# Sparse attention with a gated feed-forward on one core: first gate weights in one transfer, and the head of the written-out order rewritten

## The chip, the cores and the metric

The kernel runs on one core of a Trainium2 chip. A core has a matrix engine (TensorE, PE in the profile, with its weight loads shown apart as PEld), three engines for elementwise work (VectorE or DVE, ScalarE or ACT, GpSimd or POOL), and SyncE (SP), which here only issues transfers. Each engine has a queue of its own and runs it in order; engines wait for each other by semaphores. Sixteen DMA engines move data between the chip's memory and the core. They serve several queues; in the profile, q1 holds the transfers that SP issues and q0 those that POOL issues.

The metric is the device time of one execution in microseconds. Lower is better.

## The reference

Causal attention in which each query attends only to the six chunks of 32 keys whose scores have the highest upper bound, and then a gated feed-forward over all tokens:

```python
k_min = np.min(k_chunks, axis=3)
k_max = np.max(k_chunks, axis=3)
ub = np.sum(np.maximum(q[:, :, :, None, :] * k_min[:, :, None, :, :],
                       q[:, :, :, None, :] * k_max[:, :, None, :, :]), axis=-1)
ub = np.where(causal, ub, -1000000000.0)
top_chunks = np.argsort(ub, axis=-1)[..., -6:]
...
scores = np.where(sel & (pos[:, None] >= pos[None, :]), scale * q @ k.T, -1000000000.0)
attn = softmax(scores)
x = (attn @ v) as [3072 tokens, 512]
gate = 1 / (1 + exp(-(x @ w_gate)))
out = ((gate * (x @ w_val)) @ w_out)
```

There are 4 batches, 8 heads, 768 positions and a head dimension of 64, so x has 3072 rows of 512. The feed-forward has 1536 columns. Inputs and output are fp32; the kernel computes in fp16 with fp32 sums.

## The kernel before

The work is cut into eight units, u0 to u7, of 384 tokens each. Unit u0 takes the first 128 queries of batches 0, 1 and 2. These lie in the first four chunks, so all of their allowed chunks are selected and no choice is needed. The function `first` does them, one batch at a time, under names that end in the batch: `kf0_0`, `kf1_0` (loads of even and odd heads' keys), `qf0_0`, `qf1_0`, `vf_0`; `kfT_0`, `qfT_0` (transposes on TensorE, L709), `kf16_0`, `qf16_0` (casts), `scf_0` (scores, L746), `expf` (ACT, L751), `cmf` (causal mask on POOL, L753), `vc_1`, `vc_2` (values cast to fp16 as `vh`), `pvf` (weights times values, L760), `rzf` and `xf` (division by the sum, DVE, L766 and L768), `xpsf` (turned back, L775) and `xTf` (copied to the feed-forward's input). Unit u1 is the other half of the start, queries 128 to 511 of batch 0. Its loads (`k0_u1` to `k3_u1`, `q0_u1` to `q3_u1`, L647, one for each pair of heads) are copied (`kn`, `qn`), turned (`kT`, `qT`, L795), cast (`kt`, `qf`) and spread into per-head tiles (`hk0`, `hk1`, `hq0`, `hq1`). `kx0` and `kx1` (L681) are the minimum and maximum over each chunk, `kcr` the range between them, `qm` the positive part of the queries, `ub` the upper bounds on TensorE (L896); from them a choice is made on DVE, and then scores, exponentials and values follow as in u0. Raw values for u1 come by `v_0_1` to `v_0_3` (L667), cast on POOL by `v16`.

The tiles of keys and queries have rows of a fixed pattern that is copied into them once from `epat` (`hkp` copies, eight of them).

The feed-forward of a unit (`ffn`, L1239 to L1319) has 12 column blocks: four matmuls for the gate `g` (128x384 each, L1259), tanh on ACT, four matmuls for the value `v`, one product on DVE (`hg`, L1280), and in the end matmuls with `w_out` (`o`, L1308). u0's block starts as soon as u0's attention is done, and u1's attention is woven into it. All weights are loaded in that time, cast to fp16 by the transfer, by POOL's queue: gate, value and output weights each in three groups of four blocks (`wg0` to `wg2`, L612; `wv0` to `wv2`, L613; `wo0` to `wo2`). Only the first gate group is split: `wgp` (L610) brings the first 128 rows of its 512, and `wg0` the other 384.

At the very start and between the early steps stand 30 matmuls on a tile of ones (`fl_0` to `fl_29`, L591), whose result nobody reads; they keep TensorE occupied. Before the change, nine of them run first and the others stand between transposes up to the start of the feed-forward.

The order of all work is written out. `ORDER` is one list of about 2010 operations; each entry names an operation and its engine (`P` TensorE, `A` ACT, `V` DVE, `G` POOL, `S` SP), and each engine's queue holds its entries in the order of that list. `SLOTS` gives each buffer the place that it takes in its pool. `TIES` holds extra waits: `a<b` makes `a` wait for `b` although no data passes between them. The loop at the end of the kernel emits the operations:

```python
    for op in plan.order():
        n = len(traced)
        op.emit(op.engine)
        for b in ties.get(op.name, ()):
            tc.add_manual_dep(traced[n], ends[b], ...)
```

Loads come in the order of SP's entries. Before, they are: `k2_u1 qf1_0 kf1_0 kf0_0 kf1_2 kf0_1 qf0_0 qf1_1 kf1_1 qf0_1 vf_0 qf0_2 qf1_2 kf0_2 vf_1 k0_u1 q3_u1 q2_u1 vf_2 q1_u1 k3_u1 q0_u1 k1_u1 v_0_3 v_0_2 v_0_1 qf1_3 k0_u2 q2_u2 k1_u2`, and then the rest of u2's and batch 3's first block.

Of the kernel before, what the change touches and what calls it, by code (L numbers as in the profile page):

```python
# [401 lines left out]
def kernel(  # L402
# [201 lines left out]

    def weights(i, prio, after):
        lo, hi = 512 * i, 512 * i + 512
        c0 = 0
        if i == 0:
            c0 = 1
            plan.add("wgp", {POOL: (760, 760)}, lambda e: nc.gpsimd.dma_start(wg16[:, 0:1, lo:hi], wgs[:, 0:1, lo:hi]),  # L610
# [846 lines left out]
```

## Time and profile before

| | |
|---|---|
| median of 3 runs | 280.38 us (279.79 to 280.73) |
| the profiled execution's own time | 279.88 us |
| its span in the profile | 278.2 us |
| granted TensorE clock, mean | 1.000 of full |
| TensorE busy | 269.2 us, 97% |
| DVE, ACT, POOL busy | 231.2, 180.4, 163.1 us |
| moved by DMA | 34.70 MB, mean 125 GB/s |

The span runs from the first to the last instruction that the profile shows; the execution's time has 1.7 us more around it. "Busy" is the time in which an engine has an instruction in work, so a busy TensorE isn't one at its peak rate. A row of the groups, such as `L1259 PE MATMUL g_u<-xT_u,wg 128*128 128x384 f16 x288 | 56.0, 326 | ...`, gives line, engine, operation, output and inputs, the shape and count, total busy us, mean ns of one, and the idle time just ahead of them with what ended it. A row of the timeline gives start, length (both us), engine, line and operation, and how many of them follow each other; in brackets stands how long the engine had been idle and what released it. In the answers on waits the three numbers are the total, the times and the longest. In the chain that ended last, a row is a start, a length, and what the time was spent on. A row on transfers gives the queue, the count of issues, the size of one, and the median time from the start of its issue to its landing.

### The profile page before, as it was taken

The numbers are of one execution on the slowest core, as the hardware profiler recorded it, in microseconds if no ns is written. First come the engines' busy times: TensorE is split into PE (matmuls) and PEld (weight loads), VectorE is DVE, ScalarE is ACT, GpSimd is POOL, SyncE is SP. The second block draws the span as 40 slices with busy tenths as digits, with TensorE's granted clock in tenths as the row PEclk, the third lists the DMA queues.
The fourth block names the chain that finished last, engine by engine and source line by source line (L and its number), as shares of the span: only waits on it lengthen the run. The fifth ranks groups of instructions, "written<-read, shape, count | busy, mean of one in ns | idle before, by whom it ended". The sixth has DMA issues, their size and how long they took to land.

```text
span 278.2 us, 7566 instructions
## 1 busy us (share of the span) xinstructions
PE 269.2 (97%) x2806; PEld 189.3 (68%) x2806; DVE 231.2 (83%) x686; ACT 180.4 (65%) x386; POOL 163.1 (59%) x262
## 2 busy tenths in 40 slices
PE   5979999999999999999999999999999999999995
PEld 3755658667755666557687657776888688778684
DVE  4799747687999998796999987978889998888985
ACT  6388969569858944468689979988983422341430
POOL 5797744639372873534669966724766467163440
PEclk9999999999999999999999999999999999999999
DMA  6999999999999598696896230100320033000304
GB/s 157 258 281 204 207 217 208 220 179 202 187 217 189 142 183 188 145 161 125 164 157 114 68 85 17 40 0 3 73 77 2 1 83 127 2 1 2 151 2 152
DMA packets 131717, 34.70 MB, mean 125 GB/s; under 512 B 119776, under 2 KB 128736, under 8 KB 131680
## 3 DMA queue, kind: packets, MB, share of 16 engines
q1 hardware_dynamic: 126912, 29.50, 50.6%
q0 software_dynamic: 4768, 4.72, 10.1%
q8 instruction: 22, 0.36, 0.5%
q14 instruction: 15, 0.12, 0.1%
HBM read 30.67 MB, written 6.29 MB: 133 GB/s over the span
## 4 chain that ended last, share of the span: by engine, by line
PE 87%; DMA 6%; DVE 5%; SPq 1%; issue 0%; POOL 0%; DVEq 0%
PE v_u L1259 20%; PE g_u L1259 15%; PE sc_u L957 12%; PE o_u L1308 11%; PE p_u L1082 10%; PE pv_u L990 7%; DMA wg<-in_moe_w_gate_dram 5%; PE p_g_u L1191 5%; PE ube_u L896 3%; DMA kf<-in_k_dram 1%; DVE xf L768 1%; PE kfT L709 1%; PE qfT L709 1%; PE fl L591 1%; DVE kx_u L681 1%; DVE kcr L681 1%
## 5 line engine op out<-in xcount | busy, mean ns | idle before, releaser
L968 ACT ACTIVATE att_u<-sc_u 128x512 f16<-128x512 f32 (+3 forms) x184 | 86.9, 573 | 8.6 <-PE sc_u L957 7.3
L1259 PE MATMUL v_u<-xT_u,wv 128*128 128x384 f16 x384 | 72.4, 326 | 0.0
L1280 DVE SCALAR_TENSOR_TENSOR hg_u<-gate_u,v_u 128x384 f16<-128x384 f16 x96 | 51.2, 545 | 19.3 <-ACT gate_u L1271 9.7
L1271 ACT ACTIVATE gate_u<-g_u 128x384 f16<-128x384 f32 x72 | 35.1, 499 | 40.3 <-PE g_u L1259 35.1
L1259 PE MATMUL g_u<-xT_u,wg 128*128 128x384 f16 x288 | 56.0, 326 | 0.9 <-ACT xT_u L452 0.5
L1259 PEld LDWEIGHTS <-wv 128*128 128x128 f16 x384 | 36.2, 98 | 20.3 <-issue 0.2
L974 POOL TENSOR_SCALAR_AFFINE_SELECT att_u<-att_u 128x384 f16<-128x384 f16 (+1 forms) x56 | 28.0, 509 | 37.4 <-ACT att_u L968 16.4
L1259 PEld LDWEIGHTS <-wg 128*128 128x128 f16 x288 | 26.7, 98 | 18.3 <-DMA wg<-in_moe_w_gate_dram 1.8
L1308 PE MATMUL o_u<-wo,hg_u 128*128 128x512 f16 x144 | 34.3, 379 | 0.0
L990 PE MATMUL pv_u<-v,att_u 128*128 128x65 f16 x640 | 26.3, 193 | 0.0
L990 PEld LDWEIGHTS <-att_u 128*128 128x128 f16 x640 | 24.2, 98 | 2.9 <-issue 0.6
L1228 DVE TENSOR_TENSOR f_g_u<-p_g_u,f_g_u 128x192 f32<-128x192 f32 (+1 forms) x72 | 24.9, 383 | 1.0 <-PE p_g_u L1191 0.4
L957 PE MATMUL sc_u<-hqe,hke 128*128 128x128 f16 (+2 forms) x220 | 25.1, 243 | 0.0
L957 PE MATMUL sc_u<-hqo,hko 128*128 128x128 f16 (+2 forms) x220 | 24.1, 243 | 0.0
L1308 PEld LDWEIGHTS <-hg_u 128*128 128x128 f16 x144 | 13.7, 98 | 13.4
L957 PEld LDWEIGHTS <-hke 128*128 128x128 f16 x220 | 16.5, 98 | 4.9 <-issue 0.6
L957 PEld LDWEIGHTS <-hko 128*128 128x128 f16 x220 | 16.4, 98 | 4.4
L673 POOL CAST v<-v 128x512 f16<-128x512 f32 x23 | 14.4, 627 | 5.8 <-DVE qf_u L863 1.8
L1271 ACT ACTIVATE gate_u<-f_g_u 128x384 f16<-128x384 f32 x24 | 11.9, 519 | 5.6 <-DVE hg_u L1280 2.9
L1011 DVE TENSOR_TENSOR x_u<-pv_u,rz_u 128x384 f16<-128x384 f32 (+1 forms) x28 | 14.6, 524 | 0.9 <-DMA xT_u<-x_u 0.6
L919 DVE MAX8 mx_u<-ubn_u 128x8 f32<-128x8 f32 (+16 forms) x152 | 12.7, 158 | 0.3
L1099 DVE SCALAR_TENSOR_TENSOR sw<-p_u,sw 128x256 f32<-128x256 f32 (+1 forms) x20 | 10.6, 528 | 2.4 <-PE p_u L1082 2.0
(187 smaller groups left out, 504.9 us busy)
## 6 DMA issues: line engine op xcount, KB each, us to landing
v<-in_v_dram SPq DMA_DIRECT2D x23, 256.0 KB, 4.7
k<-in_k_dram SPq DMA_DIRECT2D x12, 384.0 KB, 5.4
q<-in_q_dram SPq DMA_DIRECT2D x12, 384.0 KB, 5.9
out_dram<-osb_u SPq DMA_DIRECT2D x12, 256.0 KB, 3.3
out_dram<-sw SPq DMA_DIRECT2D x8, 256.0 KB, 2.1
wv<-in_moe_w_val_dram POOLq DMA_DIRECT2D x3, 512.0 KB, 9.8
wo<-in_moe_w_out_dram POOLq DMA_DIRECT2D x3, 512.0 KB, 17.6
qf<-in_q_dram SPq DMA_DIRECT2D x8, 128.0 KB, 3.3
```

What stands on the lines that cost most here:

```text
L673: plan.add(f"v16_{b}_{ib}", {POOL: pool(H * D)}, lambda e: nc.gpsimd.tensor_copy(v16[b % 2][:, ib, :, 0:D], at(t)), reads=[t], writes=[("v ...
L957: nc.tensor.matmul(at(t)[:, o:o + 128 * m], hk[b % 2][e_][:, p, 128 * jb:128 * jb + 128], hq[u.side][e_][:, p, 128 * x:128 * (x + m)], sta ...
L968: plan.add(f"exp_{u.name}_{h}_{y}", {ACT: act(n)}, lambda e, t=t, att=att, b0=b0, n=n: nc.scalar.activation(at(att)[:, b0:b0 + n], at(t), ...
L974: nc.gpsimd.affine_select(out=dv, in_=dv, compare_op=ALU.is_ge, fill=0.0, base=0, pattern=[[0, u.m], [1, 128]], channel_multiplier=-1)
L990: nc.tensor.matmul(at(pv)[:, last, x, :], at(att)[:, c:c + 128], v16[b % 2][:, jb, h, :], start=(jb == 0), stop=(jb == ib))
L1011: plan.add(f"x_{u.name}_{p}", {DVE: dve(u.t)}, lambda e: nc.vector.tensor_tensor(at(x_).rearrange("p a (e d) -> p e a d", e=2), at(pv)[:, ...
L1082: nc.tensor.matmul(at(to)[:, side], a(j)[:, i], b(j)[:, i], start=j == i == 0, stop=j == 2 and i == 1)
L1228: plan.add(f"{p}_{name}", {POOL: pool2(192 * n), DVE: dve(192 * n)} if slow else {DVE: dve(192 * n)}, lambda e: both(e).tensor_tensor(dst( ...
L1259: nc.tensor.matmul(at(t), w16[:, c, 128 * fb:128 * fb + 128], at(u.xt)[:, c, :], start=(c == 0), stop=(c == 3))
L1271: plan.add(f"tanh_{u.name}_{fb}", {ACT: act(T, not seven[0])}, lambda e, gv=gv, gate=gate: nc.scalar.activation(at(gate), gv(), AF.Tanh, s ...
L1280: plan.add(f"hg_{u.name}_{fb}", {DVE: dve(T)}, lambda e, vv=vv, gate=gate, hg=hg, fb=fb: nc.vector.scalar_tensor_tensor(at(hg)[:, fb % 2], ...
L1308: nc.tensor.matmul(at(o), at(hgs[fc // 2])[:, fc % 2, 128 * tb:128 * tb + 128], wo16[:, fc, lo:hi], start=(fc == 0), stop=(fc == NFB - 1))
```

## The change

The change rewrites the first 290 or so entries of `ORDER` (the rest, 1717 entries, stays the same), renumbers `SLOTS`, adds six `TIES` and loads the first gate group in one transfer. In parts:

- **Gate weights.** `wgp` is gone; `wg0` brings all 512 rows (512 KB in fp16). The gate matmuls of the first four blocks no longer read the separate part. On POOL, `wg0` and `wv0` now stand ahead of the key copy `hkf0` and behind `cmf_1_1`, as the list shows.
- **Loads.** SP's order is now `k2_u1 kf1_2 kf0_0 kf1_0 qf1_0 qf0_1 qf0_0 qf1_1 qf1_2 qf0_2 kf0_2 kf0_1 kf1_1 vf_0 vf_1 k0_u1 q3_u1 k3_u1 v_0_2 vf_2 q2_u1 q1_u1 k1_u1 q0_u1 v_0_3 v_0_1 qf1_3 k0_u2 k1_u2 q2_u2`, and the rest as before.
- **Fillers.** 28 of the 30 matmuls on ones stand at the start of TensorE's queue, ahead of the first transpose; one follows the first key transpose and one stands ahead of `scf_1`. None is left behind that.
- **Order on TensorE.** Batch 2's first block is turned ahead of batch 1's; the feed-forward begins with `g_u0_2 g_u0_0`, then `ub_u1`, `g_u0_1 g_u0_3` and the value blocks 1, 3, 2, 0 (before: `g_u0_0 g_u0_2`, `ub_u1`, `g_u0_3 g_u0_1`, and the value blocks 1, 0, 2, 3).
- **Engines.** 28 copies and casts run elsewhere. DVE to ACT: `kt_u1_2 kf16_0 kf16_1 kn_u1_0 xTf_1_1 qf_u1_1 qf_u1_2 hkp001 hkp101 hq1_u1_0 hkf1`. DVE to POOL: `kcr_f`. ACT to DVE: `kn_u1_2 hkp110 hkp000 hk1_u1_2 hkp111 qn_u1_0 kt_u1_3 hq0_u1_2`. ACT to POOL: `qm_u1_3 qm_u1_2 hq1_u1_1`. POOL to ACT: `hk0_u1_2 hkp100 vc_2 hk0_u1_3 hq1_u1_3`.
- **Ties.** `kcr_f<rzf_2_1 hkf0<rzf_2_0 kn_u1_1<xf_2_0 qm_u1_3<kx0_u1_3 hq0_u1_3<qn_u1_0 hq1_u1_1<hq0_u1_2`, all on POOL, waiting for DVE. No old tie is gone.

The diff, without the renumbered slots and the rewrapped lists:

```diff
@@ ORDER @@
-ident=G ones16=V fl_4=P fl_2=P fl_8=P fl_3=P fl_1=P fl_0=P fl_29=P k2_u1=S kn_u1_2=A qf1_0=S kf1_0=S kf0_0=S fl_6=P fl_5=P epat0=V
-ident16=V ap0=V epat=G hkp110=A hkp000=A hkp001=V kT_u1_2=P kcr0=V kt_u1_2=V hk0_u1_2=G vf1_1=G hkp011=V hkp010=G vf1_2=G hkp100=G
-kf1_2=S kf0_1=S kfT_0=P kxf1=V fl_17=P fl_10=P fl_7=P kx0_u1_2=V kf16_0=V qf0_0=S qfT_0=P qf16_0=V qf1_1=S kf1_1=S kfT_1=P
-kf16_1=V fl_15=P fl_16=P scf_0=P expf_0_1=A fl_19=P qf0_1=S qfT_1=P hq0=V ap1=V fl_14=P fl_9=P fl_13=P fl_11=P fl_18=P fl_12=P
-qf16_1=V scf_1=P v10=G vf_0=S v16_0_0=G qf0_2=S qf1_2=S kf0_2=S expf_0_0=A cmf_0_0=G pvf_0_0=P rzf_0_0=V xf_0_0=V kx1_u1_2=V
-cmf_0_1=G wgp=G kfT_2=P pvf_0_1=P qfT_2=P qf16_2=V rzf_0_1=V xf_0_1=V kxf0=V expf_1_0=A cmf_1_0=G vf_1=S vc_1=G pvf_1_0=P
-rzf_1_0=V xpsf_0_0=P expf_1_1=A cmf_1_1=G pvf_1_1=P hkf0=G hk1_u1_2=A kf16_2=A scf_2=P expf_2_1=A expf_2_0=A k0_u1=S kn_u1_0=V
-kT_u1_0=P xf_1_0=V fl_20=P fl_21=P wg0=G q3_u1=S qn_u1_3=A q2_u1=S rzf_1_1=V xf_1_1=V xpsf_1_1=P hq1=V xTf_1_1=V kx0_u1_0=V
-kx1_u1_0=V vf_2=S wv0=G cmf_2_0=G fl_23=P xpsf_0_1=P fl_24=P fl_22=P fl_27=P xpsf_1_0=P vc_2=G xTf_1_0=V pvf_2_0=P rzf_2_0=V
-xf_2_0=V q1_u1=S k3_u1=S kn_u1_3=G kT_u1_3=P hkp111=A q0_u1=S fl_28=P kx1_u1_3=V cmf_2_1=G pvf_2_1=P xpsf_2_0=P rzf_2_1=V xf_2_1=V
-qT_u1_3=P qf_u1_3=V k1_u1=S qn_u1_1=A qT_u1_1=P xTf_0_0=A xTf_0_1=A qn_u1_2=A qn_u1_0=A kn_u1_1=G kT_u1_1=P kx1_u1_1=V kx0_u1_1=V
-kt_u1_0=A qm_u1_3=A fl_25=P xpsf_2_1=P fl_26=P qT_u1_2=P v_0_3=S v_0_2=S v_0_1=S qf1_3=S k0_u2=S q2_u2=S k1_u2=S qf_u1_1=V
-qf_u1_2=V v11=G wv1=G wg1=G hq0_u1_3=G qT_u1_0=P kt_u1_3=A hk0_u1_3=G hq1_u1_3=G wv2=G xTf_2_1=A xTf_2_0=A qf_u1_0=A qm_u1_0=A
-g_u0_0=P g_u0_2=P kx0_u1_3=V kcr_f=V kcr_u1=V hkp101=V hq1_u1_0=V hkf1=V kt_u1_1=V hk0_u1_1=G wg2=G qm_u1_2=A qm_u1_1=A ub_u1=P
-ubn0_u1=V ubm0_u1=V hq0_u1_1=A hq0_u1_2=A g_u0_3=P g_u0_1=P mx0_u1=V ap0_u1=V apt0_u1=V hqm0_u1_0=V v_u0_1=P v_u0_0=P v_u0_2=P
-hq0_u1_0=A tanh_u0_2=A tanh_u0_1=A hg_u0_1=V ubn1_u1=V v_u0_3=P tanh_u0_3=A hg_u0_3=V ubm1_u1=V hg_u0_2=V tanh_u0_0=A hg_u0_0=V
-hk0_u1_0=A hq1_u1_1=A sc_u1_0_2=P exp_u1_0_2=A sc_u1_1_2=P sc_u1_0_1=P sc_u1_0_0=P exp_u1_1_2=A sc_u1_1_0=P sc_u1_1_1=P
-exp_u1_0_0=A exp_u1_0_1=A v_u0_7=P wo0=G hqm0_u1_2=G sc_u1_2_2=P exp_u1_2_2=A sc_u1_2_0=P exp_u1_2_0=A sc_u1_3_0=P sc_u1_3_2=P
...
+ones16=V fl_23=P k2_u1=S kf1_2=S fl_4=P fl_12=P fl_10=P ident=G epat0=V epat=G hkp000=V hkp100=A hkp001=A ap0=V kn_u1_2=V v11=G
+hkp010=G kf0_0=S kf1_0=S qf1_0=S qf0_1=S fl_15=P fl_24=P fl_28=P fl_19=P fl_2=P fl_17=P fl_9=P fl_0=P fl_20=P fl_26=P fl_27=P
+fl_6=P fl_18=P fl_1=P fl_22=P fl_5=P fl_25=P fl_8=P fl_29=P fl_11=P fl_14=P fl_7=P fl_13=P fl_3=P kT_u1_2=P kt_u1_2=A hk0_u1_2=A
+fl_16=P hkp110=V hkp111=V kfT_0=P qf0_0=S qfT_0=P ident16=V qf16_0=V hkp011=V kf16_0=A scf_0=P expf_0_1=A kcr0=V hk1_u1_2=V
+kx1_u1_2=V qf1_1=S qfT_1=P cmf_0_1=G expf_0_0=A cmf_0_0=G qf1_2=S qf0_2=S qfT_2=P kf0_2=S kfT_2=P kf16_2=A kf0_1=S kf1_1=S kfT_1=P
+kf16_1=A qf16_1=V qf16_2=V fl_21=P scf_1=P expf_1_0=A vf_0=S v10=G v16_0_0=G pvf_0_0=P rzf_0_0=V pvf_0_1=P rzf_0_1=V xf_0_0=V
+xpsf_0_0=P xf_0_1=V xpsf_0_1=P vf1_1=G vf_1=S vc_1=G cmf_1_0=G pvf_1_0=P expf_1_1=A cmf_1_1=G vf1_2=G wg0=G k0_u1=S q3_u1=S
+k3_u1=S xTf_0_0=A qn_u1_3=A wv0=G scf_2=P expf_2_1=A expf_2_0=A kxf1=V kxf0=V kx0_u1_2=V rzf_1_0=V pvf_1_1=P rzf_1_1=V xf_1_1=V
+v_0_2=S vf_2=S q2_u1=S xpsf_1_1=P ap1=V xf_1_0=V xpsf_1_0=P qT_u1_3=P qf_u1_3=V hkf1=A xTf_0_1=A xTf_1_1=A cmf_2_0=G cmf_2_1=G
+vc_2=A pvf_2_1=P rzf_2_1=V pvf_2_0=P rzf_2_0=V xf_2_1=V xf_2_0=V xTf_1_0=V kn_u1_0=A kT_u1_0=P kx1_u1_0=V wv1=G kn_u1_3=G
+kT_u1_3=P kx0_u1_3=V kx1_u1_3=V kx0_u1_0=V kt_u1_3=V xpsf_2_1=P xpsf_2_0=P q1_u1=S qn_u1_1=A qT_u1_1=P hq1_u1_3=A qn_u1_2=A
+hkp101=A xTf_2_0=A qf_u1_1=A qT_u1_2=P qf_u1_2=A kt_u1_0=A xTf_2_1=A qm_u1_1=A kcr_f=G k1_u1=S hkf0=G kn_u1_1=G kT_u1_1=P wg1=G
+qm_u1_3=G q0_u1=S qn_u1_0=V qT_u1_0=P qf_u1_0=A qm_u1_0=A g_u0_2=P g_u0_0=P wv2=G hq0_u1_3=G qm_u1_2=G kx1_u1_1=V hq0=V kx0_u1_1=V
+kcr_u1=V ub_u1=P kt_u1_1=V hq0_u1_2=V ubn0_u1=V ubm0_u1=V hq0_u1_0=A wg2=G hq1_u1_1=G mx0_u1=V ap0_u1=V apt0_u1=V hqm0_u1_0=V
+hk0_u1_0=A g_u0_1=P g_u0_3=P hq1_u1_0=A v_u0_1=P tanh_u0_1=A hg_u0_1=V ubn1_u1=V hq0_u1_1=A tanh_u0_3=A v_u0_3=P hg_u0_3=V
+ubm1_u1=V v_u0_2=P tanh_u0_2=A hg_u0_2=V hq1=V v_u0_0=P tanh_u0_0=A hg_u0_0=V hk0_u1_3=A sc_u1_0_2=P exp_u1_0_2=A hk0_u1_1=G
+sc_u1_1_2=P sc_u1_0_1=P sc_u1_0_0=P exp_u1_1_2=A sc_u1_1_0=P sc_u1_1_1=P exp_u1_0_0=A exp_u1_0_1=A v_u0_7=P wo0=G hqm0_u1_2=G
...
@@ TIES, first line of the new list @@
+kcr_f<rzf_2_1 hkf0<rzf_2_0 kn_u1_1<xf_2_0 qm_u1_3<kx0_u1_3 hq0_u1_3<qn_u1_0 hq1_u1_1<hq0_u1_2 hqm0_u1_2<hqm0_u1_0 v16_0_3<hg_u0_1
...
@@ -604,13 +604,8 @@
 
     def weights(i, prio, after):
         lo, hi = 512 * i, 512 * i + 512
-        c0 = 0
-        if i == 0:
-            c0 = 1
-            plan.add("wgp", {POOL: (760, 760)}, lambda e: nc.gpsimd.dma_start(wg16[:, 0:1, lo:hi], wgs[:, 0:1, lo:hi]),
-                     writes=[("wg", 0, "first")], prio=prio, dma=(750, 2048))
-        return plan.add(f"wg{i}", {POOL: (760, 760)}, lambda e: nc.gpsimd.dma_start(wg16[:, c0:, lo:hi], wgs[:, c0:, lo:hi]),
-                 reads=after, writes=[("wg", i)], prio=prio, dma=(750 * (4 - c0), 2048)), plan.add(f"wv{i}", {POOL: (760, 760)}, lambda e: nc.gpsimd.dma_start(wv16[:, :, lo:hi], wvs[:, :, lo:hi]),
+        return plan.add(f"wg{i}", {POOL: (760, 760)}, lambda e: nc.gpsimd.dma_start(wg16[:, :, lo:hi], wgs[:, :, lo:hi]),
+                 reads=after, writes=[("wg", i)], prio=prio, dma=(3000, 2048)), plan.add(f"wv{i}", {POOL: (760, 760)}, lambda e: nc.gpsimd.dma_start(wv16[:, :, lo:hi], wvs[:, :, lo:hi]),
                  reads=after, writes=[("wv", i)], prio=prio, dma=(3000, 2048))
 
@@ -1265,7 +1260,7 @@
             else:
                 g = ps(f"g_{u.name}_{fb}", "ff", [128, T])
                 gv, gk = lambda g=g: at(g), [g]
-                op = plan.add(f"g_{u.name}_{fb}", pe(650), product(g, wg16), reads=xt + [("wg", fb // 4)] + [("wg", 0, "first")] * (fb < 4), writes=[g],
+                op = plan.add(f"g_{u.name}_{fb}", pe(650), product(g, wg16), reads=xt + [("wg", fb // 4)], writes=[g],
                               prio=next_())
                 plan.hold(op, gate)
             plan.add(f"tanh_{u.name}_{fb}", {ACT: act(T, not seven[0])}, lambda e, gv=gv, gate=gate: nc.scalar.activation(

```

220 lines of the change are left out of this document (110 added, 110 removed).

## The prediction

> **What bounds the kernel now.** I read the page's shares first, then busy time by stretch, then what TensorE waits for in the first 50 us, and then the early rows one by one.
>
> ```profile
> span 278.2 us, 7566 instructions
> PE 269.2 (97%) x2806; PEld 189.3 (68%) x2806; DVE 231.2 (83%) x686; ACT 180.4 (65%) x386; POOL 163.1 (59%) x262
> ```
> ```profile
> 14.00:18.00 4.00, 2.39 (x32) 1.65 (x31) 3.65 (x12) 2.83 (x6) 4.00 (x7) 1.00 1.14 298
> 18.00:23.00 5.00, 4.05 (x40) 3.10 (x37) 4.93 (x14) 4.95 (x12) 4.79 (x11) 1.00 1.25 233
> 23.00:40.00 17.00, 16.88 (x156) 10.25 (x155) 12.06 (x49) 13.20 (x33) 9.60 (x17) 1.00 1.21 209
> 40.00:60.00 20.00, 19.75 (x216) 13.05 (x215) 14.47 (x54) 13.87 (x36) 10.32 (x21) 1.00 1.12 206
> ```
> ```profile
> PE g_u L1259 <- ACT xT_u L452: 0.5, 1, 0.5
> PE g_u L1259 <- DMA wg<-in_moe_w_gate_dram: 0.2, 1, 0.2
> ```
>
> The first line of the page's shares is busy time. In the rows by stretch, columns after the stretch and its length are busy us of PE, weight load, DVE, ACT and POOL, then clock, DMA share, GB/s. TensorE is busy 97% of the span and has almost no hole after 23 us, so what the change can move is when the first feed-forward block (unit u0) begins on it, and any hole that it opens or shuts later. The order of the work after the first 290 operations is the same in both kernels. Only three things of the new head reach past 23 us: the start of that block, the landings of the weights, and the landings of the loads queued behind them. The one wait still shown there, 0.2 us, is for the last gate weights. Between 14 and 23 us four engines are all nearly full, POOL 4.00 of 4.00, DVE 4.93 of 5.00: whatever is put there displaces something.
>
> **The change, part by part.**
>
> *Gate weights in one transfer.* POOL issues them:
>
> ```profile
> 12.82 0.79 POOL L610 DMA_DIRECT2D wg<-in_moe_w_gate_dram  x1
> 13.63 0.66 POOL L753 TENSOR_SCALAR_AFFINE_SELECT attf<-attf 128x512 f16<-128x512 f16 x1
> 14.21 0.63 POOL L456 CAST vh<-vf 128x512 f16<-128x512 f32 x1
> 14.77 0.64 POOL L753 TENSOR_SCALAR_AFFINE_SELECT attf<-attf 128x512 f16<-128x512 f16 x1
> 15.35 0.61 POOL L456 COPY hke<-kf 64x512 f16<-64x512 f16 x1
> 15.91 0.80 POOL L612 DMA_DIRECT2D wg<-in_moe_w_gate_dram  x1
> ```
> ```profile
> wg<-in_moe_w_gate_dram POOLq DMA_DIRECT2D x1, 128.0 KB, 5.5
> ```
> ```profile
> wg<-in_moe_w_gate_dram POOLq DMA_DIRECT2D x1, 384.0 KB, 7.3
> ```
>
> The small issue (0.79 us of POOL) goes, and the key copy `hkf0` (0.61) moves behind the big issue. Floor: 15.91 - 0.79 - 0.61 = 14.5 us. Between lie the value cast and two mask steps, which now also depend on the earlier score matmuls, so I take 14.7, that is 1.2 us sooner. The transfer grows from 384 to 512 KB. Rates of the two DMA queues come from three windows, 15.5 to 16.3, 20.4 to 22.4, and 23 to 40 us (packets, MB, share):
>
> ```profile
> q1 hardware_dynamic: 208, 0.15, 63.3%
> q0 software_dynamic: 64, 0.06, 50.6%
> ```
> ```profile
> q0 software_dynamic: 396, 0.39, 120.2%
> ```
> ```profile
> q0 software_dynamic: 2498, 2.48, 85.9%
> q1 hardware_dynamic: 2877, 1.04, 34.5%
> ```
>
> Queue q0, which carries the weights in 1 KB packets, moves 396 / 2.0 = 198 a us alone and 2498 / 17 = 147 a us beside a full q1, which then gets 169. So 128 packets more take 0.65 to 0.87 us. Landing: 15.91 + 7.3 = 23.2 before; now 23.2 - 1.2 + 0.65 to 0.87 = 22.7 to 22.9, or up to 23.4 if q1, less drained by then, holds it at the lower rate throughout. The lead of 1.2 us is thus mostly eaten.
>
> By the Trainium skill (DMA: Bandwidth & Descriptors, Anatomy of one DMA) a software-queue transfer takes about 2.0 us plus bytes over 436 GB/s, an estimate of 3.2 us for 512 KB, and the weights would lie ready by 18 us. The trace disagrees, with 7.3 us for 384 KB and 5.5 us for 128 KB.
>
> *Order of the loads and fillers.* First scores may begin when `kfT_0` and `qfT_0` are through; the fillers between them are gone, and 28 run at the very start instead of 9.
>
> ```profile
> 1.12 2.10 PE L591 MATMUL fl<-ones 128*128 128x256 f16 x9 [1.12 <-DVE ones L587]
> 5.81 1.09 PE L709 MATMUL kfT<-ident,kf 128*128 128x128 f32 x4 [0.90 <-DMA kf<-in_k_dram]
> 9.28 0.63 PE L591 MATMUL fl<-ones 128*128 128x256 f16 x2
> 12.43 0.40 PE L746 MATMUL scf<-qf,kf 64*128 64x128 f16 x8
> 12.89 0.63 PE L709 MATMUL kfT<-ident,kf 128*128 128x128 f32 x4
> ```
>
> Nine fillers take 2.10 us, so about 0.21 us each at the slow early rate: 28 end at 1.12 + 28 x 0.21 = 7.0, or about 6 if the rate rises on the way. The key transpose moves from 5.81 to 6.2 - 7.0, but its partner, the query transpose, waits for a load landing at 7.4 in both orders, so nothing is lost. Batch 0's scores then come about 1.2 us sooner; batch 1's, whose second key load is now 13th in the queue, only 0.6 us (12.43 to 11.8). That feeds the 14.7 above.
>
> *28 casts.* These rows decide the start:
>
> ```profile
> 18.53 0.55 DVE L681 TENSOR_REDUCE kx_u<-kT_u 128x12 f32<-128x384 f32 x1
> 19.39 0.42 DVE L768 TENSOR_TENSOR xf<-pvf,rzf 128x256 f16<-128x256 f32 x1
> 20.04 0.93 ACT L452 COPY qn_u<-kq_u 128x384 f32<-128x384 f32 x2
> 21.50 0.82 PE L795 MATMUL qT_u<-ident,qn_u 128*128 128x128 f32 x6
> 22.13 0.65 ACT L452 COPY xT_u<-xpsf 128x256 f16<-128x256 f16 x2
> 22.20 1.01 DVE L454 COPY qf_u<-qT_u 128x384 f32<-128x384 f32 x2
> 22.82 1.76 PE L1259 MATMUL g_u<-xT_u,wg 128*128 128x384 f16 x8 [0.51 <-ACT xT_u L452]
> ```
>
> DVE gives eleven to ACT and one to POOL and takes eight from ACT; POOL gives five to ACT and takes three. At some 0.5 us each that is 2 us off DVE, 1 us off POOL and 2.5 us more on ACT, which had 4.95 of 5.00 busy from 18 to 23 but only 2.83 of 4.00 before. Among the ones moved is `qn_u1_0`, the query copy that now ends last, from ACT to DVE. I walk the new order engine by engine with the durations of the trace, each step starting when its engine and its inputs are free; steps follow each other 0.08 us before the one in front is written. ACT ends the last `xT` at 22.4 - 22.6 (22.78 before). DVE is busy without a pause from 17.7, when the first query transpose reaches it: one query cast, four chunk extremes and one key cast at 0.47 net (2.8), two reciprocals and two divisions (1.1), one `xT` (0.3), so `qn_u1_0` runs from 17.7 + 4.2 = 21.9 to 22.5; its transpose (0.5 us) leaves TensorE at 22.5 - 22.9, and the feed-forward starts behind it, about 22.85. Before, it started at 22.82 with its four first-quarter matmuls and then met the late weights at 23.2, losing 0.1. The query bounds follow at 24.15 instead of 24.5. So TensorE gains 0.1 to 0.35 here if the weights land by 22.9, and loses 0.2 to 0.3 if they land at 23.4. I take a gain of 0.2.
>
> The six new waits make POOL's `kcr_f`, `hkf0`, `kn_u1_1`, `qm_u1_3`, `hq0_u1_3` and `hq1_u1_1` stand behind DVE steps; behind them on POOL wait the issues of `wg1`, `wv2` and `wg2`.
>
> ```profile
> 26.18 14.22 DMA wg<-in_moe_w_gate_dram
> 40.45 1.48 PE g_u L1259 x8
> ```
>
> `wg2` is issued at 26.18 and lands at 40.40, with several transfers ahead of it, so issues a microsecond late cost nothing; they would cost their lateness if q0 ran dry. What sets `wg2` is when q0 starts and its rate. It starts 1.2 us sooner with 128 packets more in front (0.87 us): `wg2` lands 0.3 us sooner, at 40.1. If q1 is no longer idle in 20.4 to 22.4, q0 loses 2.0 x (198 - 147) = 102 packets, 0.7 us, and it lands at 40.8. With TensorE there at 40.45 - 0.25 - 0.2 = 40.0, the matmul starts between 40.1 and 40.85 instead of 40.45. I take 40.35: of the 0.2 gained at the start, 0.1 is left. From there TensorE has no hole in before, and the end moves as this matmul moves.
>
> *The loads behind.* q1 pays for weights that start sooner. The first row is q1 between 17.0 and 20.3 us; the others are the load with the least room, its use, and the matmuls behind it.
>
> ```profile
> q1 hardware_dynamic: 2444, 0.80, 95.2%
> ```
> ```profile
> kq_u<-in_k_dram SPq DMA_DIRECT2D x1, 128.0 KB, 14.2
> ```
> ```profile
> 34.06 1.75 SPq L647 DMA_DIRECT2D kq_u<-in_k_dram  x1
> 50.00 0.41 ACT L452 COPY kn_u<-kq_u 128x256 f32<-128x256 f32 x1
> 51.37 0.50 PE L795 MATMUL kT_u<-ident,kn_u 128*128 128x128 f32 x3
> ```
>
> In that stretch q1 moves 2444 / 3.3 = 740 packets a us; beside a busy q0 it gets 169. 1.2 us of earlier q0 cost it 1.2 x (740 - 169) = 685 packets. Against this the early small transfer is gone, which held q1 for its 128 / 80 = 1.6 us (64 / 0.8 = 80 a us of q0, in 15.5 to 16.3) at 260 instead of some 400 a us, which I estimate from its 63.3% share at 260 (260 / 0.633 = 411): 1.6 x 140 = 225. So q1 falls 460 packets behind, 460 / 169 = 2.7 us for every load behind. But it idles for 2.0 us before 22.4; if the lag fills that idle, 2.0 x 169 = 340 packets are regained and 0.7 us remain. The tightest load lands at 34.06 + 14.2 = 48.3 and is used at 50.0, so it has 1.7 us: a lag of 0.7 is hidden, one of 2.7 makes `kn_u2_3` 1.0 us late, and its transposes at 51.37 stall TensorE for up to 1.0. Bounds 0 and 1.0; I take 0.2, near the lower, since SP issues the late loads when earlier ones land and the idle is just where the lag arises.
>
> **Sum.** -0.1 at the last gate weights, +0.2 for the loads: +0.1 on 279.88, the profiled execution's own time, 279.98. The median of the three runs is 280.38, 0.5 above it, so 280.5.
>
> **The rivals.**
>
> *The clock falls back.* The rows above show TensorE slow until 9.28 (a key transpose of four takes 1.09) and fast at 12.89 (0.63). It was fast only behind a dense stretch of fillers and scores from 10.5 on; 8 us of transposes with holes had not made it so. Before, ten fillers stand between batch 2's scores and the feed-forward; now there are none, TensorE has holes of 1.8 us near 15 and 2.0 us near 21 by my walk, and beside them mostly transposes. If the clock falls, transposes take 1.7 times as long and the first feed-forward matmuls twice their 0.185 us (1.48 / 8 in the row at 40.45), until it rises again. A rise took dense work of more than 2.1 us (the nine fillers, with slow transposes behind them) and at most 12.89 - 9.28 = 3.6 us. Of that time at half speed half is lost: 1.05 to 1.8, less the 0.2 that the wait for `wg2` takes in, and up to 0.5 for slow transposes ahead: +0.9 to +2.1, so 281.2 to 282.4, middle 281.9. Against it: before, TensorE was busy only 2.39 of 4.00 from 14 to 18 us, much of it in transposes, and was fast behind it. The point that decides: the first g matmuls spaced 0.3 us or more. Chance 0.18. The Trainium skill (TensorE: Matmul & The Clock Gate, Part 4, on transposes) says that transposes do not count as busy for the clock, which speaks against this change; its section on why this matters asks only for no holes over about 3 us, which the walk keeps.
>
> *Loads late.* The full lag of 2.7 us, with 1.0 us stalled at `kT_u2`: 280.38 - 0.1 + 1.0 = 281.3; decides when the load lands after 50.0. The late rows of batch 3's first block follow it and could add 0.3. Chance 0.17.
>
> *Faster.* Weights at 22.7, start of the block gains 0.35, `wg2` at 40.1 and TensorE there at 39.9, loads hidden: 280.38 - 0.35 = 280.0; with the ACT and DVE ends 0.2 sooner still and the 0.2 wait gone, 279.5. Over 0.3% (0.84 us) needs both ends at their best. Chance 0.1.
>
> *The change does nothing.* Everything in front of 22.8 is hidden behind landings: 280.4. It shares the middle with my forecast.
>
> **How the numbers follow.** 0.3% is 0.84 us, about what a measurement can tell here: 279.54 to 281.22. Forecast with the do-nothing case 0.55, nearly all within; clock 0.18, nearly all slower; late loads 0.17, two thirds slower; faster 0.1, of which two thirds pass the bound. Slower 0.18 + 0.11 + 0.04 from the forecast's upper tail = 0.33; faster 0.09 with its lower tail; same 0.58. Range: low 279.5 from the faster rival's best, high 282.2 inside the clock rival, which leaves out about 0.1 above and 0.05 below. The forecast alone: 279.9 to 281.1.
>
> **What would show it.** `wg0` issued at 14.4 - 14.9 and landed at 22.6 - 23.4; first g matmul at 22.7 - 23.1 behind the query transpose; the last gate weights at 40.1 - 40.9; `k3` of the third unit at 49.0 - 51.0; g matmuls spaced under 0.19 from the first. Wrong would be: slow transposes near 20 us, a TensorE hole over 0.5 us between 23 and 53, or a `wg0` later than 23.6.

## The result and the profile after

The changed kernel takes 285.17 us (median of 4 runs, 282.19 to 286.15), the kernel before 280.41 (4 runs, 279.79 to 280.73). The ratio is 1.014, with a 95% interval of 1.010 to 1.018: slower by 1.4%. Medians here and below are of all runs; ratios leave out the few runs that lie over 1.5% above the fastest of the same kernel. The changed kernel varies over 4 us from run to run, the one before over 1 us here and over almost 4 us (279.85 to 283.60) in one of the later rounds. The profiled execution took 285.58 us, 5.70 more than the 279.88 of the one before.

The page's first lines, and then busy time by stretch (columns as in the prediction), for the changed kernel:

```profile
span 283.9 us, 7573 instructions
PE 271.0 (95%) x2806; PEld 190.9 (67%) x2806; DVE 229.5 (81%) x682; ACT 184.0 (65%) x391; POOL 163.3 (58%) x260
```
```profile
14.00:18.00 4.00, 2.21 (x28) 1.48 (x26) 2.81 (x9) 3.70 (x9) 4.00 (x8) 0.82 1.01 208
18.00:23.00 5.00, 2.21 (x19) 1.97 (x18) 3.85 (x11) 0.81 (x3) 1.30 (x3) 0.80 1.15 221
23.00:30.00 7.00, 5.25 (x19) 3.00 (x20) 2.68 (x7) 6.52 (x14) 5.42 (x8) 0.53 1.23 216
30.00:40.00 10.00, 10.00 (x98) 6.03 (x97) 6.87 (x35) 6.94 (x18) 5.65 (x10) 0.99 1.22 206
```

Between 18 and 23 us, where TensorE had been busy 4.05 of 5.00 us and the other three engines at least 4.79, TensorE is now busy 2.21, ACT 0.81 and POOL 1.30: they wait. Between 23 and 30 us the granted clock is 0.53. From 30 us on TensorE is as full as before. Below stand its three longest waits up to 60 us, then the waits of the other engines for loads, and then rows of the chain that ended last:

```profile
PE qT_u L790 <- ACT qn_u L452: 3.3, 2, 2.8
PE xpsf L770 <- DVE xf L763: 2.4, 3, 1.3
PE qT_u L790 <- DVE qn_u L454: 1.2, 1, 1.2
```
```profile
ACT qn_u L452 <- DMA kq_u<-in_q_dram: 4.2, 1, 4.2
DVE qn_u L454 <- DMA kq_u<-in_q_dram: 4.6, 1, 4.6
POOL kn_u L456 <- DMA kq_u<-in_k_dram: 5.1, 1, 5.1
```
```profile
12.35 2.44 SPq L642
15.86 10.52 DMA kq_u<-in_q_dram
26.50 0.57 DVE qn_u L454
27.11 0.90 PE qT_u L790 x3
28.02 2.45 PE g_u L1254 x8
```

The query copies of the second unit (`qn_u1_1` on ACT, `qn_u1_0` on DVE) and a key copy (`kn_u1_1` on POOL) wait 4 to 5 us for their loads. The last of these, `q0_u1`, is issued at 15.86 and lands at 26.38. Before, it was issued at 13.43 and took 5.4 us:

```profile
kq_u<-in_q_dram SPq DMA_DIRECT2D x1, 192.0 KB, 5.4
```

That is a landing at 18.8, so it comes 7.6 us later. Of these, 2.4 are lost at the issue: SP stands 2.44 us at the issue of `q2_u1` (the first row of the chain), right behind `v_0_2` and `vf_2`. The other 5.1 are lost in the transfer. The feed-forward starts right behind the landing. In the timeline:

```profile
14.30 1.00 POOL L607 DMA_DIRECT2D wg<-in_moe_w_gate_dram  x1
27.81 2.66 PE L1254 MATMUL g_u<-xT_u,wg 128*128 128x384 f16 x8
```

The start moves from 22.82 to 27.81 us: 5.0 of the 5.7 us. Its first eight matmuls take 2.66 us, at half clock, instead of 1.76: 0.9. The short wait for the last gate weights, near 40 us, is gone: -0.25. That sums to 5.6.

Why does a load that was issued at 16 us take ten? The two DMA queues between 17 and 19 us (packets, MB, share), first before, then after:

```profile
q1 hardware_dynamic: 1721, 0.62, 116.9%
q0 software_dynamic: 9, 0.01, 2.7%
```
```profile
q0 software_dynamic: 214, 0.22, 70.8%
q1 hardware_dynamic: 206, 0.16, 31.7%
```

Before, the weights' queue q0 all but paused in these two microseconds, between the small transfer and the rest, and q1 sent 1721 packets. Now `wg0`, `wv0` and `wv1` follow each other on q0 without a pause, q1 gets about one packet for each of q0's, and sends 206, with 0.16 MB in place of 0.62.

### The profile page after: what moved, and what is told of

Same layout as the page of the kernel before. It is cut to its first block, busy times and chain, and to the rows that moved or that the text cites. A ratio compares the mean times of both kernels' runs of the same rounds, so it can differ in the third digit from the quotient of the medians.

```text
span 283.9 us, 7573 instructions
## 1 busy us (share of the span) xinstructions
PE 271.0 (95%) x2806; PEld 190.9 (67%) x2806; DVE 229.5 (81%) x682; ACT 184.0 (65%) x391; POOL 163.3 (58%) x260
## 4 chain that ended last, share of the span: by engine, by line
PE 92%; DMA 4%; SPq 1%; DVE 1%; issue 0%; DVEq 0%
PE v_u L1254 22%; PE g_u L1254 17%; PE sc_u L952 12%; PE o_u L1303 11%; PE p_u L1077 9%; PE pv_u L985 7%; PE p_g_u L1186 5%; DMA kq_u<-in_q_dram 4%; PE ube_u L891 3%; PE fl L591 2%; SPq L642 1%; PE qfT L704 1%; PE qT_u L790 1%; PE kfT L704 1%; PE kT_u L790 0%; PE ubo_u L891 0%
## 5 line engine op out<-in xcount | busy, mean ns | idle before, releaser
L1254 PE MATMUL g_u<-xT_u,wg 128*128 128x384 f16 x288 | 57.0, 331 | 0.0
L1254 PEld LDWEIGHTS <-wv 128*128 128x128 f16 x384 | 36.2, 98 | 20.3 <-issue 0.2
L1254 PEld LDWEIGHTS <-wg 128*128 128x128 f16 x288 | 27.3, 99 | 17.4 <-issue 2.7
L668 POOL CAST v<-v 128x512 f16<-128x512 f32 x23 | 14.4, 628 | 6.1 <-DVE qf_u L858 1.8
```

Source lines behind the costliest of these rows:

```text
L668: plan.add(f"v16_{b}_{ib}", {POOL: pool(H * D)}, lambda e: nc.gpsimd.tensor_copy(v16[b % 2][:, ib, :, 0:D], at(t)), reads=[t], writes=[("v ...
L1254: nc.tensor.matmul(at(t), w16[:, c, 128 * fb:128 * fb + 128], at(u.xt)[:, c, :], start=(c == 0), stop=(c == 3))
```

## The experiments

In the diffs below a move within the list is shown as the entry at its old and new place, and `...` stands for entries left out. Each ratio is to the kernel before as it ran in the same round, with medians of 280.68 to 281.09 us.

**e1: the value load back behind the queries.**

```diff
 @@ ORDER @@
-v_0_2=S vf_2=S q2_u1=S
+vf_2=S q2_u1=S
...
-q0_u1=S qn_u1_0=V
+q0_u1=S v_0_2=S qn_u1_0=V
```

> The changed kernel with one load moved: v_0_2 goes behind q0_u1 on SP, as before the change. Loads theory (the weights' queue starts while q1_u1, k1_u1 and q0_u1 are still waiting behind v_0_2 and vf_2, and then takes every second packet): the three leave SP about 1.5 to 2.5 us sooner, q0_u1 lands at 21 to 23 instead of 26.4, the feed-forward starts at 23.5 to 24.5 instead of 27.8, and the time falls to 281 to 282.5. Clock theory (the slow TensorE from 16.4 to 30.4 is the loss, and the late loads lie beside it): the time stays at 284.5 to 285.5.

Measured: 282.63 us median, ratio to before 1.006 (1.003 to 1.009); the profiled run 282.05. `q0_u1` is issued at 14.06 and lands at 19.7, sooner than the 21 to 23 expected, and the feed-forward starts at 23.59; the median lies just above the 282.5 expected. TensorE's gate matmuls, and its waits from 20 to 45 us:

```profile
23.59 1.47 PE L1252 MATMUL g_u<-xT_u,wg 128*128 128x384 f16 x8 [0.74 <-ACT qf_u L450]
```
```profile
PE g_u L1252 <- ACT qf_u L450: 0.7, 1, 0.7
PE pv_u L983 <- POOL att_u L967: 0.6, 1, 0.6
```

One entry on SP's queue brings 3.5 of the 5.7 us back between the profiled runs and 2.5 of 4.8 between the medians, and the intervals of the two ratios don't overlap. That speaks against the theory that the loss was the clock with the late loads beside it. The clock fell here too, to 0.50 from 15.6 to 22.4 us, but it was back at 1.00 for the first gate matmuls (1.47 us instead of 2.66), so 1.2 us of the gain come by way of the clock. The new 0.6 us is a wait that the start had covered: POOL stands at the cast of `v_0_1`, which lands at 36.2, with the masks for `pv_u` behind it.

```profile
36.33 0.61 POOL L666 CAST v<-v 128x512 f16<-128x512 f32 x1 [3.10 <-DMA v<-in_v_dram]
37.47 0.42 PE L983 MATMUL pv_u<-v,att_u 128*128 128x65 f16 x8 [0.60 <-POOL att_u L967]
```

**e2 and e3: matmuls on ones put back into the holes, alone and with e1.**

```diff
 @@ ORDER, 31 new entries @@
+(8 fillers) xpsf_1_1=P ... (3) xpsf_1_0=P ... (12) qT_u1_1=P ... (2) qT_u1_2=P ... (6) qT_u1_0=P
-    for i in range(30):
+    for i in range(61):
         keep_awake(i)
```

> The changed kernel with 31 more matmuls on ones, put ahead of xpsf_1_1, xpsf_1_0, qT_u1_1, qT_u1_2 and qT_u1_0, where TensorE waits in the changed kernel. Clock theory: the granted clock stays at 1.00 from 14 to 31 us and the first eight gate matmuls take 1.3 to 1.5 us instead of 2.66; the time falls by the slow matmuls and bounds behind 27.8, 1.5 to 2.5 us, to 282.5 to 283.5. Loads theory alone: the first feed-forward matmul stays at 27 to 28 us and the time at 284.5 or more.

> Both edits together, v_0_2 behind q0_u1 and the 31 matmuls in the holes. If the two causes add up and are all of it: the feed-forward starts at 23 to 24.5 at full clock and the time is 280 to 281.5, within 0.3% or a little over the kernel before. If something else of the change costs (ties, the 28 casts): 282 or more.

Measured: 289.56 and 288.62 us, ratios 1.029 (1.025 to 1.034) and 1.029 (1.022 to 1.036). Both missed, through the way that they were built. The timeline of e2:

```profile
15.01 2.54 PE L591 MATMUL fl<-ones 128*128 128x256 f16 x8
20.96 4.05 PE L591 MATMUL fl<-ones 128*128 128x256 f16 x12
```

Each group's fillers shared one place in the accumulator memory but were buffers of their own, and one followed another only after 0.33 us: 31 of them take 10 us, not 3.4, and that is more than the holes hold. At that spacing they didn't keep the clock either: it fell to 0.50 near 24 us. So neither run decides between the theories.

**e5 and e6: the same, as one operation of several matmuls on one buffer.**

```diff
+    def keep_more(i, count):
+        t = ps(f"fg_{i}", "pr", [128, 2, 128])
+        def several(e):
+            for _ in range(count):
+                nc.tensor.matmul(at(t), ones16, ...)
 @@ ORDER @@
+(10 matmuls) xpsf_1_1=P ... (3) xpsf_1_0=P ... (8) qT_u1_1=P ... (2) qT_u1_2=P ... (5) qT_u1_0=P
```

e5 is this on the changed kernel, e6 on e1.

> The changed kernel with 28 more matmuls on ones at the same five places as in e2, but each place is one group that writes one buffer, so that they follow each other at 0.11 us instead of the 0.33 us of e2, where each waited for the one before in its bank. Clock theory: clock 1.00 from 14 to 23 us; it may fall in the rest of the hole that the late load leaves behind 22; the time falls by 1 to 2.5 us, to 282.5 to 284.5. Loads theory alone: 285 or more, the feed-forward still at 27 to 28 us.

> The changed kernel with v_0_2 behind q0_u1 (as in e1) and the grouped matmuls of e5. If early loads and clock are the two causes and add up: feed-forward at 22.8 to 23.7 at full clock, 280 to 281.5. If the stall behind 36 us that e1 showed (the value load v_0_1 landing at 36 instead of 30) goes on, 0.6 us more than before remains: 281 to 281.8. If something else of the change costs, 282 or more.

Measured: e5 285.58 us, ratio 1.016 (1.011 to 1.021); e6 283.96, ratio 1.011 (1.006 to 1.016). In e6 the clock stays at 1.00 from start to end of the stretch, where the changed kernel had 0.57 and 0.54. First the changed kernel, then e6, in the same stretches:

```profile
16.30:20.30 4.00, 3.41 (x25) 2.82 (x23) 2.83 (x10) 1.93 (x5) 3.00 (x6) 0.57 1.03 182
22.90:30.40 7.50, 5.66 (x21) 3.02 (x21) 2.68 (x7) 6.96 (x15) 5.77 (x9) 0.54 1.23 216
```
```profile
16.30:20.30 4.00, 3.45 (x34) 2.38 (x32) 3.21 (x10) 3.90 (x8) 4.00 (x8) 1.00 0.98 191
22.90:30.40 7.50, 6.62 (x66) 3.51 (x65) 4.94 (x21) 5.14 (x12) 3.93 (x6) 1.00 1.22 198
```

And yet neither is measurably faster than its kernel without them. The profiled run of e5 is the fastest of its four (284.14 us): `q0_u1` happened to land at 24.5 there, and the feed-forward started at 25.62, not at the 27 to 28 us of the loads theory. The profiled run of e6 is the slowest of its four (285.51 us). In it the next waits come up, the first behind the late load `v_0_1`, the second on a transfer:

```profile
PE pv_u L994 <- POOL att_u L978: 2.4, 1, 2.4
PE g_u L1263 <- DMA wg<-in_moe_w_gate_dram: 0.9, 1, 0.9
```
```profile
15.88 22.60 DMA v<-in_v_dram
38.60 0.61 POOL v L677
39.21 0.49 POOL att_u L978
```

`v_0_1` takes 22.6 us to land. Ready engines help little while late loads set three points one behind the other: the queries of the second unit, the first gate weights, and the last value block. The clock theory by itself doesn't hold: the clock did fall, but holding it up gained nothing that these runs can measure while the loads were late. A gain as small as the 0.9 us found at the first gate matmuls would lie within their intervals.

**e4: the fillers at the start, on the kernel before.**

```diff
 @@ ORDER of the kernel before: 21 entries moved @@
+ident=G ones16=V (fl_4 to fl_26, all 30)=P k2_u1=S ...
```

> The kernel before with one part of the change: all 30 matmuls on ones stand at the start of TensorE's queue, none later. Clock theory: the granted clock falls to about 0.5 between 15 and 23 us and stays there for some us of the feed-forward: 282 to 283.5. If the clock fell only for the holes that the late loads opened: no fall, 280 to 281.

Measured: 282.03 us, ratio 1.003 (1.002 to 1.005). This part costs 0.3% alone. In two stretches, 14 to 23 and 23 to 31 us, the clock's column has 0.69 and 0.80, where before has 1.00 in both:

```profile
14.00:23.00 9.00, 6.84 (x57) 5.38 (x57) 7.36 (x23) 6.85 (x14) 8.45 (x16) 0.69 1.18 263
23.00:31.00 8.00, 8.00 (x70) 5.20 (x69) 7.01 (x26) 5.83 (x15) 4.58 (x8) 0.80 1.22 216
```

The clock falls, and none of the waits listed for TensorE's matmuls in this trace is for a load. But the run doesn't price the clock: the feed-forward starts at 25.43, 2.6 us later than before, and ahead of it TensorE waits 2.7 us for DVE's query casts. Slow transposes and early steps delayed behind 30 fillers can't be parted here.

**e7 and e8: two parts of the change, each alone on the kernel before.** e7 puts `v_0_2` forward, e8 loads the first gate group in one transfer ahead of `hkf0`.

```diff
 @@ e7, ORDER of the kernel before @@
-q3_u1=S qn_u1_3=A q2_u1=S
+q3_u1=S v_0_2=S qn_u1_3=A q2_u1=S
```
```diff
 @@ e8, ORDER of the kernel before, and weights() as in the change @@
-cmf_0_1=G wgp=G kfT_2=P
+cmf_0_1=G kfT_2=P
...
-pvf_1_1=P hkf0=G ... fl_21=P wg0=G
+pvf_1_1=P wg0=G hkf0=G ... fl_21=P
```

> The kernel before with one part of the change: the value load v_0_2 stands behind q3_u1, ahead of the loads of the second unit that are still missing. Loads theory: 1024 packets of 256 bytes more stand ahead of q2, q1, k3, q0 and k1; they land 1 to 3 us later, k3_u1 and k1_u1 (0.15 and 0.47 us of room) hold up the start, and the time is 281 to 283. If it takes the earlier weights too to make the loads late: within 0.5 us of before.

> The kernel before with one part of the change: the first gate group in one transfer, issued ahead of hkf0, so at about 14.5 us. The weights' queue starts at 16.3 as in the changed kernel, but the loads stand in the old order, with the three values last. Loads theory: q0_u1 and k1_u1 land 0.5 to 2 us later than 18.8 and 19.4; the time is 280.5 to 282. If the early weights alone make the loss: k1_u1 lands at 22 or later and the time is 283 or more. If weights are what the start waits for: 279.5 to 280.2.

Measured: 281.52 us, ratio 1.002 (0.999 to 1.004), and 281.61, ratio 1.002 (0.999 to 1.005). Neither is clear of no change. The medians lie within the loads theory's bounds (281 to 283, 280.5 to 282), but in e8 its step missed: `q0_u1` and `k1_u1` land at 17.6 and 18.9, sooner than before (18.8 and 19.4), not 0.5 to 2 us later. The runs of e8 that count for the ratio spread from 279.84 to 283.27. Its profiled run, 282.76 us, is one of the slower ones, and shows what can happen:

```profile
24.34 1.47 PE L1252 MATMUL g_u<-xT_u,wg 128*128 128x384 f16 x8 [2.21 <-DMA wg<-in_moe_w_gate_dram]
```

The weights are issued 1.5 us sooner than before and land at 24.30, 1.1 us later than the 23.2 before: q0 starts while q1 still has its value loads, sends 97 packets from 17 to 19 us beside 887 of q1, and then some 150 a us instead of the 198 that it moves alone.

Do the parts add up? Alone on the kernel before they cost 0.2, 0.2 and 0.3%, and 0.4 to 0.5% is left for the new order and the casts in e11 and e13 below. That is 1.1 to 1.2% against 1.4%, a gap within the noise of these runs. That early weights hurt more with the value load ahead is suggested by e1, where moving that load back brings 0.8%, while moving it forward costs 0.2% (0 to 0.4) in e7. The traces fit: `q0_u1` lands at 26.4 with both changes, at 19.7 without the value load ahead in e1, and at 19.3 with it but without the early weights in e7. The two together on the kernel before were not run.

**e9: the weights three microseconds later.** If an earlier start of q0 is the cause, a later one must gain.

```diff
 @@ ORDER of the changed kernel @@
-vf1_2=G wg0=G k0_u1=S ... qn_u1_3=A wv0=G scf_2=P
+vf1_2=G k0_u1=S ... qn_u1_3=A scf_2=P
...
-cmf_2_1=G vc_2=A
+cmf_2_1=G wg0=G wv0=G vc_2=A
```

> The changed kernel with wg0 and wv0 moved on POOL's queue to behind cmf_2_1, so that the first weights are issued at about 17.3 instead of 14.3. Loads theory, as the traces so far sharpen it: SP's queue sends 400 to 1000 packets a us alone and some 140 beside the weights' queue, and what it has left when the weights begin decides; with weights that begin 3 us later the last load of the second unit lands at 20 to 22 instead of 26.4, the feed-forward starts at 24 to 25.5 in spite of weights issued later, and the time falls by 2 to 3.5 us, to 281.5 to 283.5. If early weights are worth anything: the weights land 3 us later, the start doesn't come sooner, 285 or more.

Measured: 284.0 us, ratio 1.008 (1.005 to 1.012), 1.2 us under the changed kernel, by intervals that overlap (1.010 to 1.018), and less than the 2 to 3.5 expected. So the gain in time isn't clear of noise, but the trace shows the mechanism: `q0_u1`, issued at 15.81 as late as in the changed kernel, lands at 19.8 instead of 26.4, and the feed-forward starts at 24.73, right behind the weights.

```profile
wg<-in_moe_w_gate_dram POOLq DMA_DIRECT2D x1, 512.0 KB, 7.5
```
```profile
24.73 1.72 PE L1252 MATMUL g_u<-xT_u,wg 128*128 128x384 f16 x5 [0.18 <-DMA wg<-in_moe_w_gate_dram]
```

Issued at 17.18, they take 7.5 us; issued at 14.30 they took 9.6. Of 2.9 us of delay, 0.8 reaches the landing (24.7 against 23.9). All ten runs of e9 have mean clocks of 0.970 to 0.982, so the slow stretch is still there; in the profiled run the first eight gate matmuls take 2.21 us.

**e10, e11 and e13: how much comes back.** e10 is e6 with the weights of e9. e11 is e6 with the split of before, `wgp` ahead of `vf1_1`, `wg0` and `wv0` behind `cmf_2_0`. e13 is e11 with these two behind `cmf_2_1`.

```diff
 @@ e11, ORDER, with weights() of before @@
+wgp=G vf1_1=G vf_1=S vc_1=G
...
-cmf_1_1=G vf1_2=G wg0=G
+cmf_1_1=G vf1_2=G
-cmf_2_0=G cmf_2_1=G
+cmf_2_0=G wg0=G wv0=G cmf_2_1=G
 @@ e13 @@
-cmf_2_0=G wg0=G wv0=G cmf_2_1=G
+cmf_2_0=G cmf_2_1=G wg0=G wv0=G
```

> As e6 (v_0_2 behind q0_u1, grouped matmuls in the holes) with the weights later as in e9. If what SP's queue has left when the weights begin is the cause of the stall at 37 to 40 us in e6 too (the value load v_0_1 crawls beside the weights): that stall falls from 2.4 us to under 1, the first gate group lands at 24 to 25 and sets the start, 281 to 282.5. If the stall has another cause, it stays at 2 us or more: 284 or more.

> As e6, with the first gate group split again: wgp issued at about 12, wg0 with three quarters and wv0 at 16.7 or later, behind cmf_2_0, so that the weights' queue pauses while SP's queue sends its last loads, as before the change. If loads, pause and clock are all that the change cost, and its casts and other moves nothing: first gate group landed at 23 to 24, no stall over 1 us behind it, 280 to 281.2. If the casts, ties and the rest of the load order cost by themselves: over 281.5.

> As e11, with wg0 and wv0 one place further back on POOL's queue, behind the second mask cmf_2_1, for which TensorE waited 1.5 us at 17.9 in e11. If that wait was all that e11 had over before ahead of the feed-forward (it started at 25.1 instead of 22.8): start at 23.5 to 24.3, 281 to 282. If POOL only hands the delay on to the weights (issued 0.7 us later than 17.06, landed at 24.8 instead of 24.15): start at 25 again, 282 to 283.

Measured: e10 283.65 us, ratio 1.007 (1.003 to 1.011); e11 282.55, ratio 1.004 (1.001 to 1.008); e13 282.12, ratio 1.005 (1.003 to 1.008). e10 lies between its two expectations: the 2.4 us wait of `pv_u` is gone, but in its profiled run, the slowest of ten (284.84 us), the feed-forward starts at 25.5 and waits of 0.5 to 0.6 us for weights and an engine stand at its start and behind it. With the weights split as before the change, the clock held up and the value load at its old place (e11 and e13), no run shows more than 283.7 us, and no wait over 0.2 us is left between the start of the feed-forward and 200 us. e11 is above its bound of 281.5, and e13 between its two, with a start of the feed-forward at 24.57, 1.75 us behind that of before. Its first gate matmuls, and TensorE's waits from 12 to 40 us:

```profile
24.57 1.46 PE L1268 MATMUL g_u<-xT_u,wg 128*128 128x384 f16 x8
```
```profile
PE kT_u L804 <- POOL kn_u L453: 1.2, 1, 1.2
PE xpsf L784 <- DVE xf L777: 0.7, 1, 0.7
PE scf L755 <- ACT kf L449: 0.6, 1, 0.6
PE pvf L769 <- ACT vh L449: 0.5, 1, 0.5
```

These are waits for engines, not for loads. The casts `kf16_1` and `vc_2` (0.6 and 0.5) are two of the 28, moved to ACT. The largest, a key copy on POOL at 19.48 whose load had landed at 14.7, stands behind three issues of weights, two of which e13 put there. So by this trace a part of the remaining 0.4 to 0.5% is in the new order and places of the casts, and a part in how e13 was put together; no run parts them.

**e12: the 28 casts alone, on the kernel before.**

```diff
 @@ ORDER of the kernel before: letters of 28 entries @@
-kn_u1_2=A ... kt_u1_2=V ... vc_2=G ... qn_u1_0=A
+kn_u1_2=V ... kt_u1_2=A ... vc_2=A ... qn_u1_0=V
```

> The kernel before with one part of the change: the 28 copies and casts run on the changed kernel's engines, all else (order, loads, matmuls on ones, split weights, no new ties) as before. If the casts cost nothing by themselves, as the prediction had it: the feed-forward starts at 22.5 to 23.5 and the time is within 0.8 us of before. If they cost: ACT, which takes five casts more on balance and was full from 18 to 23 us, ends its last one later, the feed-forward starts at 24 or later and the time is 1 us or more above before.

Measured: 287.73 us, ratio 1.023 (1.019 to 1.027). The feed-forward starts at 29.5. TensorE's waits from 15 to 40 us:

```profile
PE g_u L1257 <- ACT xT_u L450: 2.6, 1, 2.6
PE kT_u L793 <- ACT kn_u L450: 1.6, 1, 1.6
PE ube_u L894 <- ACT qm_u L693: 1.3, 1, 1.3
```

ACT is late at each. In the old order the moved casts cost 7 us; in the new one, by the trace of e13, they cost a part of the 1.75 us at its start. Their own price in the changed kernel can't be told from these two.

**e14: the kernel before, with the first gate group split in halves.**

```diff
-            c0 = 1
+            c0 = 2
-... wg16[:, 0:1, lo:hi], wgs[:, 0:1, lo:hi]
+... wg16[:, 0:2, lo:hi], wgs[:, 0:2, lo:hi]
```

> The kernel before with the first gate group split in halves instead of a quarter and the rest. The small transfer ends 0.7 to 1 us later inside the pause of the weights' queue (17 to 19 us), the second carries 128 packets less and lands at 22.4 to 22.9 instead of 23.2. If the pause has room for it: same to 0.4 us faster than before. If the second transfer's place in the queue is what counts, or the last loads crawl for those 128 packets: 0 to 1 us slower.

Measured: 281.75 us, ratio 1.004 (1.001 to 1.007). Here the mechanism stands alone: 128 packets of weights more in the small transfer, as many less in the large one, and no other edit. `k3_u1` lands at 19.8 instead of 18.5, `q0_u1` at 20.9 instead of 18.8, TensorE waits for a key copy, and the feed-forward starts at 24.09 instead of 22.82:

```profile
PE kT_u L795 <- POOL kn_u L456: 1.3, 1, 1.3
```

None of the fourteen kernels is faster than the one before.

## Why the prediction was wrong, step by step

- **The step that failed: the loads behind.** In its part "The loads behind", the prediction saw that weights which start sooner put q1 behind, and sized it at 460 packets and up to 2.7 us. It laid that lag on the third unit's loads, with 1.7 us of room for the tightest, and left out that `q1_u1`, `k1_u1` and `q0_u1` were still in q1 when q0 began. These had no room (`k1_u1` is used by a POOL copy half a microsecond behind its landing), and they lead to the feed-forward's first matmul. Measured: `q0_u1` 7.6 us later, `v_0_1` at 39.6 instead of 30.1. Three different edits show the cause: e1 and e14 in the time, e9 in the landing of `q0_u1`.
- **The walk's inputs.** "DVE is busy without a pause from 17.7" and "`qn_u1_0` runs from 17.7 + 4.2 = 21.9" took its load as landed. It waited for it until 26.5. Had the walk asked of each copy when its load lands, with SP's new order, it would have met `v_0_2` and `vf_2` ahead of the last three loads: at the issue, where 2.4 us were lost, and in q1.
- **The pause.** The prediction took q0 as starting 1.2 us sooner. What counted was that the small transfer (packets from 15 to 17 us) and the rest (from 19 us) had a hole between them, in which q1 sent 1721 packets in 2 us. The window from 17.0 to 20.3 us that the prediction used for q1 hints at it in its row for q0, which the prediction doesn't show: 139 packets in 3.3 us, where q0 alone moves 198 in one (below). In one transfer the hole is gone, so in effect q0 became busy for good some 3 us sooner, not 1.2. This is the mis-sized term: with 3 us the prediction's own sum gives 3 x (740 - 169) - 225 = 1490 packets and, at 169 a us, an estimate of 8.8 us; `v_0_1` came 9.5 us later.

```profile
q0 software_dynamic: 139, 0.14, 26.6%
```

- **The gate weights.** Issue at 14.4 to 14.9 was forecast; it was 14.30. Landing at 22.6 to 23.4 was forecast; it was 23.9, since q0 moved 107 packets a us from 17 to 19 us (214 packets in 2 us, in the section on the result), below the 147 of the lower bound. The lead was not "mostly eaten" but more than eaten.
- **The clock, a rival at 0.18.** It came true: 0.50 from 16.6 to 20.0 us, after a hole of 1.3 us, not of 2, and again from 23.4 to 30.1 (between the two TensorE was nearly idle, and the column shows 1.00). The Trainium skill (TensorE: Matmul & The Clock Gate, Part 4, on transposes) has transposes not count as busy; the trace agrees, since TensorE was busy 3.41 of 4.00 from 16.3 to 20.3, all but 0.60 of it in transposes, at 0.57. The same page of the Trainium skill (Why this matters for your kernels) asks for no idle gaps over some 3 us, and by that alone this order, with a longest hole of 2.8 us near 21, would be safe; here the measurement decides. Of the size, +0.9 to +2.1 us, the 0.9 us at the first gate matmuls is the lower end; no run prices the clock by itself. But it was priced as a rival to late loads, and both happened together.
- **The sum.** +0.1 us was forecast and +4.8 measured between the medians. The rival of late loads (+1.0) had the right queue and the wrong victim. The range's upper end of 282.2 left out both happening at once. Two counts in the prediction are off by one, without weight in the sum: nine fillers, not ten, stood between batch 2's scores and the feed-forward, and POOL takes four casts, with `kcr_f` from DVE, not three.
- **What held.** From the first gate matmul on the two kernels run alike: 252.1 us from there to TensorE's end before, 252.8 after, with the 0.9 us of slow clock in it. The six new ties cost no wait that the trace names between 17 and 31 us.

Open stays what the casts cost in the new order by themselves, what the clock alone costs, and why runs of one kernel differ by up to 4 us.

## What to carry to other kernels

Here two DMA queues shared the engines and took turns packet by packet, and a transfer issued earlier was paid for by everything still waiting in the other queue. So ask what that queue still holds at the moment when the first one starts, and who uses it first. Each step in a walk through a new order needs its load's new issue and landing, not only its engine's free time. And a mean rate over a window can hide the pause that made it work.
